# Top-k attention with two expert layers: the masks of six more heads move from VectorE to ScalarE

## Chip, cores and metric

One core of a Trainium2 chip runs the whole program. The metric is the device time of one execution in microseconds (us); lower is better.

## What is computed

The reference is attention that keeps only the 32 largest scores of each row, and then two dense layers with experts:

```
scores = q @ k^T / 8                              # 2 batches, 8 heads, 576 rows, head size 64
kth    = the 32nd largest score of each row
p      = exp(score - row max) where score >= kth, else 0
x      = (p / sum(p)) @ v                         # 1152 tokens x 512
x      = sum over 4 experts e: gate[:, e] * (relu(x @ w1[e]) @ w2[e])     # 512 -> 1024 -> 512
out    = max(x @ m1, x @ m2, x @ m3) @ mo                                 # 512 -> 768 -> 512
```

All of it is float32.

## The kernel before

**Attention.** The 1152 tokens are nine tiles of 128 rows; the heads go by twos, so there are 36 pairs, numbered here from 0 as in the code (the change's description counts from 1). A pair has a first head (j = 0) and a second head (j = 1). For each head TensorE makes scores (line 420 or 425), ScalarE copies them out of PSUM into `s` (line 432), and VectorE counts the 32 largest in seven instructions: four MAX8 into `m` (line 445), each giving eight values, and three MATCH_REPLACE8 into `work` (line 447). ScalarE keeps minus the maximum as `nb` (line 452).

**The mask** is lines 459 to 485. A head that ScalarE does not mask first has its whole row exponentiated by ScalarE (line 459, `p<-s,nb`). Then VectorE compares, multiplies and sums in one instruction (line 473, `p<-s,m,p`, with both tensors in SBUF). A head that is listed in `ON_ACT` has no line 459; ScalarE makes the mask in three activations instead (lines 466, 467, 468) and an accumulator read: a leaky slope that leaves scores at or above the 32nd nearly at zero and makes the others hugely negative after the exp's scale, a [128,1] bias, and the exp with its sum. Before the change `ON_ACT` has all first heads from pair 2 on, and the second heads of pairs 2, 5 and 6. The second heads of pairs 0, 1 and 4 are masked by GpSimd, the other thirty by VectorE.

**After the mask** TensorE transposes `p` (lines 491 and 496, tile `psp`), ScalarE copies the result out (lines 494, 499, tile `pt`), `rs` gets a small guard (line 504), VectorE takes the reciprocal `rr` (line 510), ScalarE spreads it (`rb`, line 514), TensorE transposes that (`psr`, line 519) and multiplies with v (`psv`, lines 533 and 536), VectorE multiplies the two into `xt` (line 543), ScalarE rounds `xt` to `xh` (line 556) and GpSimd makes the rest `xl` (line 557).

**The dense layers** run each product in three passes of split operands (lines 682, 683, 684). A weight block arrives as `raw`; ScalarE rounds it to `whi` (line 271) and GpSimd subtracts to get `wlo` in two halves (line 277). Hidden tiles `h` are split by ScalarE and VectorE (lines 824, 826), every fourth by ScalarE and GpSimd (lines 817 to 819).

**What sets the order.** Every engine runs its own instructions in the order in which the program issues them. The program is written in slots: pair n starts at slot 8n, its first head counts in slots 8n to 8n+6, its second `stag` slots later. A set of offsets (`FIRST`, `MIDDLE`, `TIGHT`, `SECOND`, `THIRD`, `LOOSE`, chosen by `options(n)`, line 566) says in which slot each step is issued. Pairs from 8 on use `LOOSE`, only pair 11 uses `THIRD`. In `LOOSE` VectorE's mask of the second head is in slot 8n+11 and ScalarE's mask of the first head in 8n+9 (`MASK_LATE` = 2). After each slot the dense layers, the filler of TensorE, are issued until their estimated TensorE time has caught up with the estimated VectorE time of the slots so far (`clock`); the mask on VectorE adds about 0.67 us to that estimate (`dve(S)`, line 472), and a mask on ScalarE adds none. TensorE's work in all is the same however it is divided between slots.

Of the kernel before, what the change touches and what calls it, by code (L numbers as in the profile page):

```python
# [31 lines left out]
ON_POOL = ((0, 1), (0, 1, 4))  # L32
W_AHEAD = 4
WIDE, W_FROM, W_STEP = 4, 306, 2
ON_ACT = (range(2, 36), (2, 5, 6))
STEEP = 2.0 ** 100
MASK_LATE = 2

FIRST = dict(stag=2, new=1, scores=-12, trans=11, pv=17, rec=16, lag=2, sum=4, late=1)
MIDDLE = dict(stag=2, new=1, scores=-12, at=(11, 12), pv=14, rec=12, lag=1, sum=0, late=1)  # L40
TIGHT = dict(stag=3, new=1, scores=-7, at=(10, 11), guard=11, rec=11, spread=12, pv=12, turn=12, norm=13, split=13, last=14, lag=0, lag_s=1, sum=0, late=1)
SECOND = dict(TIGHT, norm=14, split=14, last=15)
THIRD = dict(stag=4, new=1, scores=-4, at=(11, 12), guard=12, rec=13, spread=13, pv=14, turn=14, norm=15, split=15, last=16, lag=0, lag_s=2, sum=0)
LOOSE = dict(stag=4, new=1, scores=-4, trans=10, pv=17, rec=15, lag=2, sum=0)

EARLY = 7
# [13 lines left out]
def kernel(  # L60
# [15 lines left out]
    B, HP, D, _, S = k.shape  # L76
# [34 lines left out]
    at = ctx.enter_context(tc.tile_pool(name="at", bufs=2))  # L111
# [287 lines left out]
    class Pair:  # L399
        def __init__(self, n):  # L400
# [8 lines left out]
            self.on_pool = [n in ON_POOL[j] for j in range(2)]  # L409
            self.on_act = [n in ON_ACT[j] for j in range(2)]  # L410

# [147 lines left out]
    def attention():  # L559
# [3 lines left out]
        later, between = {}, {}  # L563

        def options(n):
            return TIGHT if n == HP - 1 else SECOND if n == 2 * HP - 1 else MIDDLE if n in (HP - 2, 2 * HP - 3, 2 * HP - 2) else FIRST if n < 2 * HP else THIRD if n == 3 * HP - 1 else LOOSE

        def at_slot(s, f, *a):
            later.setdefault(s, []).append((f, a))
# [3 lines left out]
        for n, (c, hp, t) in enumerate(pairs):  # L573
            for b in batches(t):
                if ("v", b, hp) not in first_use:
                    first_use["v", b, hp] = n
                    at_slot(8 * n + (options(n)["pv"] - 7 if b and hp else 0), load_v, b, hp)
                if t >= FULL:
                    first_use.setdefault(("k", b, hp), n)
            if t >= FULL:  # L580
                first_use.setdefault(("q", c, hp), n)
            elif n:
                o = options(max(0, n - 2))
                at_slot(max(8 * n + options(n)["scores"] - LOAD_FULL, 8 * (n - 2) + o["scores"] + o["stag"] + 1), load_full, n)
        free = {"k": -99, "q": -99}
        for key, n in first_use.items():
# [4 lines left out]
            at = max(s0 + options(n)["scores"] - (SPLIT_K if key[0] == "k" else SPLIT_Q), free[key[0]] + 2)  # L591
            if key[0] == "k" and key[1] and key[2]:

                at = max(at, 8 * pairs.index((MIXED, key[2] - 1, MIXED)) + options(n)["scores"] + options(n)["stag"] + (1 if key[2] == HP - 1 else 4))
# [3 lines left out]
        for n, (c, hp, t) in enumerate(pairs):  # L598
# [7 lines left out]
            for j in range(2):  # L606
# [9 lines left out]
                late = o.get("late", MASK_LATE) * pr.on_act[j]  # L616
# [40 lines left out]
    lag = []  # L657
# [439 lines left out]
```

## Time and profile before

| | us |
|---|---|
| median of three executions | 767.23 |
| lowest and highest of them | 760.99, 768.05 |
| the profiled execution, its own time | 766.07 |
| its span, first to last instruction | 764.2 |
| TensorE (PE) busy in the span | 731.3 |
| VectorE (DVE) busy | 621.3 |
| ScalarE (ACT) busy | 488.5 |
| GpSimd (POOL) busy | 462.3 |

How to read the rows: a row of the order of time gives the start in us from the span's start, how long it took, the engine, the line, the operation, output<-inputs with their sizes, and in brackets how long the engine had been idle in front of it and what ended that. PEld is TensorE's weight load, which runs beside matmuls. PEclk is the TensorE clock that was granted, 1.00 being 2.4 GHz and 0.50 being 1.2 GHz. A row of a stretch gives its ends, its length, and the busy time of PE, PEld, DVE, ACT and POOL, each with its number of instructions, then PEclk, the share of time that the DMA engines were busy, and GB/s. The attention lasts to about 462 us; behind it dense layers alone are left.

### The profile page before, as it was taken

The numbers are of one execution on the slowest core, as the hardware profiler recorded it, in microseconds if no ns is written. First come the engines' busy times: TensorE is split into PE (matmuls) and PEld (weight loads), VectorE is DVE, ScalarE is ACT, GpSimd is POOL, SyncE is SP. The second block draws the span as 40 slices with busy tenths as digits, with TensorE's granted clock in tenths as the row PEclk, the third lists the DMA queues.
The fourth block names the chain that finished last, engine by engine and source line by source line (L and its number), as shares of the span: only waits on it lengthen the run. The fifth ranks groups of instructions, "written<-read, shape, count | busy, mean of one in ns | idle before, by whom it ended". The sixth has DMA issues, their size and how long they took to land.

```text
span 764.2 us, 13550 instructions
## 1 busy us (share of the span) xinstructions
PE 731.3 (96%) x4678; PEld 644.8 (84%) x4678; DVE 621.3 (81%) x1172; ACT 488.5 (64%) x1109; POOL 462.3 (60%) x401
## 2 busy tenths in 40 slices
PE   6899999699999998999999999999999999999998
PEld 3576788588899897988998877899998899999996
DVE  6999989959999899999999996999999954233341
ACT  4668888647888885987885756576555633433431
POOL 2514789449989885796975405677686742442520
PEclk9999999889999999999999999999999999999999
DMA  7683565425755534354452666878877752453501
GB/s 217 186 268 139 159 194 151 132 63 172 199 149 166 166 118 144 102 165 152 145 152 90 204 251 234 277 241 280 259 260 227 241 172 85 135 183 97 192 2 42
DMA packets 56485, 130.14 MB, mean 170 GB/s; under 512 B 9761, under 2 KB 23329, under 8 KB 56417
## 3 DMA queue, kind: packets, MB, share of 16 engines
q1 hardware_dynamic: 48064, 120.69, 50.2%
q10 hardware_dynamic: 8352, 8.59, 3.2%
q8 instruction: 37, 0.61, 0.3%
q14 instruction: 32, 0.25, 0.1%
HBM read 120.60 MB, written 8.65 MB: 169 GB/s over the span
## 4 chain that ended last, share of the span: by engine, by line
PE 65%; DVE 17%; ACT 8%; issue 5%; POOL 4%; DMA 0%; ACTq 0%; POOLq 0%; DVEq 0%
PE ps L682 16%; PE ps L684 16%; PE ps L683 16%; DVE m L445 8%; DVE work L447 6%; PE psv L536 2%; POOL wlo L277 2%; PE pss L425 2%; ACT whi L271 2%; PE psp L491 2%; PE pso L683 2%; PE pso L682 2%; PE psa L767 2%; PE pso L684 2%; PE pss L420 1%
## 5 line engine op out<-in xcount | busy, mean ns | idle before, releaser
L277 POOL TENSOR_TENSOR wlo<-raw,whi 128x512 fp32r<-128x512 f32 x228 | 305.7, 1368 | 107.5 <-ACT whi L271 102.8
L271 ACT ACTIVATE whi<-raw 128x1024 fp32r<-128x1024 f32 x148 | 152.6, 1056 | 33.3 <-POOL narrow L248 16.3
L682 PE MATMUL ps<-xl,whi 128*128 128x256 f32 (+1 forms) x520 | 160.5, 309 | 0.2
L684 PE MATMUL ps<-xh,wlo 128*128 128x256 f32 (+1 forms) x520 | 156.6, 301 | 0.1
L683 PE MATMUL ps<-xh,whi 128*128 128x256 f32 (+1 forms) x520 | 156.4, 301 | 0.0
L445 DVE MAX8 m<-work 128x8 f32<-128x576 f32 x216 | 155.1, 744 | 0.1
L447 DVE MATCH_REPLACE8 work<-m,work 128x576 f32<-128x576 f32 x144 | 106.6, 741 | 0.0
L682 PEld LDWEIGHTS ps<-xl,whi 128*128 128x128 f32 x520 | 98.4, 189 | 1.9 <-POOL xl L557 0.6
L683 PEld LDWEIGHTS ps<-xh,whi 128*128 128x128 f32 x520 | 97.8, 188 | 1.3 <-issue 0.7
L684 PEld LDWEIGHTS ps<-xh,wlo 128*128 128x128 f32 x520 | 97.6, 188 | 0.3 <-POOL wlo L277 0.3
L277 DVE TENSOR_TENSOR wlo<-raw,whi 128x1024 fp32r<-128x1024 f32 x34 | 55.1, 1622 | 48.8 <-ACT whi L271 35.9
L682 PE MATMUL ps<-wlo,h 128*128 128x512 f32 x160 | 67.7, 423 | 7.5 <-POOL wlo L277 7.5
L248 POOL TENSOR_TENSOR narrow<-narrow,raw 128x256 int32<-128x256 int32 x48 | 47.1, 982 | 38.0 <-DVE narrow L245 13.0
L684 PE MATMUL ps<-whi,h 128*128 128x512 f32 x160 | 64.3, 402 | 2.0 <-POOL h L819 2.0
L683 PE MATMUL ps<-whi,h 128*128 128x512 f32 x160 | 64.0, 400 | 0.0
L432 ACT ACTIVATE s<-pss 128x288 f32<-128x288 f32 x144 | 51.2, 401 | 14.6 <-PE pss L420 11.3
L445 DVE MAX8 m<-s 128x8 f32<-128x576 f32 x72 | 53.8, 748 | 5.5 <-ACT s L432 5.5
L447 DVE MATCH_REPLACE8 work<-m,s 128x576 f32<-128x576 f32 x72 | 53.3, 741 | 0.0
L494 ACT ACTIVATE pt<-psp 128x512 f32<-128x512 f32 x72 | 42.7, 594 | 12.2 <-PE psp L491 11.9
L491 PE MATMUL psp<-ident,p 128*128 128x128 f32 x288 | 43.8, 281 | 5.4 <-POOL p L477 4.1
L684 PE MATMUL ps<-x2h,wlo 128*128 128x384 f32 x144 | 48.7, 338 | 0.0
L682 PE MATMUL ps<-x2l,whi 128*128 128x384 f32 x144 | 48.7, 338 | 0.0
(118 smaller groups left out, 1616.1 us busy)
## 6 DMA issues: line engine op xcount, KB each, us to landing
raw<-in_w_dram SPq DMA_DIRECT2D x112, 512.0 KB, 4.2
raw<-narrow SPq DMA_DIRECT2D x36, 512.0 KB, 3.4
whole<-in_w_dram SPq DMA_DIRECT2D x30, 512.0 KB, 5.9
raw<-in_m_dram SPq DMA_DIRECT2D x36, 256.0 KB, 4.3
narrow<-narrow ACTq DMA_DIRECT2D x48, 128.0 KB, 4.3
kraw<-in_k_dram SPq DMA_DIRECT2D x16, 288.0 KB, 4.5
qraw<-in_q_dram SPq DMA_DIRECT2D x48, 64.0 KB, 3.8
raw<-in_mo_dram SPq DMA_DIRECT2D x12, 256.0 KB, 4.1
```

What stands on the lines that cost most here:

```text
L248: nc.gpsimd.tensor_tensor(out=out.bitcast(I32), in0=out.bitcast(I32), in1=last, op=ALU.add)
L271: nc.scalar.activation(out=hi, in_=raw, func=AF.Copy)
L277: on.tensor_tensor(out=lo[:, x], in0=raw[:, x], in1=hi[:, x].bitcast(F32), op=ALU.subtract)
L425: nc.tensor.matmul(ps[:, 0:SH], lhsT=l, rhs=r, start=i == 0, stop=i == len(mm) - 1)
L432: nc.scalar.activation(out=s[:, h, :], in_=halves[h][:, 0:SH], func=AF.Copy)
L445: nc.vector.max(m[:, 8 * r:8 * r + 8], src)
L447: nc.vector.match_replace(out=self.w[j], in_to_replace=m[:, 8 * r:8 * r + 8], in_values=src, imm_value=NEG)
L491: nc.tensor.transpose(ps[:, r * P:(r + 1) * P], self.p[:, part, part * TAIL + r * P:part * TAIL + (r + 1) * P], ident)
L494: return lambda: [nc.scalar.activation(out=d, in_=ps.rearrange("p (r n) -> p r n", r=NR), func=AF.Copy), self.did.add(("pt", part))]
L682: nc.tensor.matmul(ps, lhsT=lh, rhs=rl, start=first, stop=False)
L683: nc.tensor.matmul(ps, lhsT=lh, rhs=rh, start=False, stop=False)
L684: nc.tensor.matmul(ps, lhsT=ll, rhs=rh, start=False, stop=last)
```

## The change

Six second heads are added to `ON_ACT`: those of pairs 8, 9, 10, 12, 13 and 14. These pairs get a set of offsets of their own, `BOTH`. It is `LOOSE` with `late=1`, so that both masks are issued one slot later than a VectorE mask would be (first head in slot 8n+8, formerly 8n+9; second head in 8n+12, formerly 8n+11 on VectorE), and the transposes stay where they were (`at=(13, 14)`). Pairs 11 and 15 keep their VectorE masks. The added line moves every later line number by one.

```diff
-ON_ACT = (range(2, 36), (2, 5, 6))
+ON_ACT = (range(2, 36), (2, 5, 6, 8, 9, 10, 12, 13, 14))
...
+BOTH = dict(stag=4, new=1, scores=-4, at=(13, 14), pv=17, rec=15, lag=2, sum=0, late=1)
 LOOSE = dict(stag=4, new=1, scores=-4, trans=10, pv=17, rec=15, lag=2, sum=0)
...
         def options(n):
-            return TIGHT if n == HP - 1 else SECOND if n == 2 * HP - 1 else MIDDLE if n in (HP - 2, 2 * HP - 3, 2 * HP - 2) else FIRST if n < 2 * HP else THIRD if n == 3 * HP - 1 else LOOSE
+            return TIGHT if n == HP - 1 else SECOND if n == 2 * HP - 1 else MIDDLE if n in (HP - 2, 2 * HP - 3, 2 * HP - 2) else FIRST if n < 2 * HP else THIRD if n == 3 * HP - 1 else BOTH if n in ON_ACT[1] else LOOSE
```

VectorE's order around the mask of pair 10's second head (`m_1500` before, `m_1493` after), before:

```order
L445 MAX m_1500<-work 128x8
L826 SCALAR_TENSOR_TENSOR h<-ps_1570,h 128x512
L447 MATCH_REPLACE work<-m_1602,work 128x576
L473 SCALAR_TENSOR_TENSOR p,rs<-s,m_1500,p 128x576
L445 MAX m_1702<-s 128x8
L445 MAX m_1602<-work 128x8
L543 TENSOR_TENSOR xt<-psv,r 128x128
```

After:

```order
L446 MAX m_1493<-work 128x8
L448 MATCH_REPLACE work<-m_1561,work 128x576
L446 MAX m_1673<-s 128x8
L446 MAX m_1561<-work 128x8
L544 TENSOR_TENSOR xt<-psv,r 128x128
L827 SCALAR_TENSOR_TENSOR h<-ps_1595,h 128x512
```

The mask between the last count of the head and `xt` is gone, and one split of a hidden tile has moved behind `xt`.

ScalarE's order at the same place, from the last `whi` ahead of `xh` to the mask of pair 11's first head (`m_1602` before, `m_1561` after), before:

```order
L271 ACTIVATE whi<-raw 128x1024
L556 ACTIVATE xh<-xt 128x128
L504 ACTIVATE rs<-rs 128x2
L452 ACTIVATE nb<-m_1702 128x1
L432 ACTIVATE s<-pss 128x288 x2
L494 ACTIVATE pt<-psp 128x512
L514 ACTIVATE rb<-rr 128x128
L494 ACTIVATE pt<-psp 128x512
L499 ACTIVATE pt_1742<-psp 128x128
L466 ACTIVATE s<-s,m_1602 128x576
```

After:

```order
L272 ACTIVATE whi<-raw 128x1024
L825 ACTIVATE h<-ps_1595 128x512
L467 ACTIVATE s<-s,m_1493 128x576
L468 ACTIVATE nb<-m_1493,nb 128x1
L469 ACTIVATE p,rs<-s,nb 128x576
L557 ACTIVATE xh<-xt 128x128
L272 ACTIVATE whi<-raw 128x1024
L505 ACTIVATE rs<-rs 128x2
L453 ACTIVATE nb<-m_1673 128x1
L433 ACTIVATE s<-pss 128x288 x2
L495 ACTIVATE pt<-psp 128x512
L515 ACTIVATE rb<-rr 128x128
```

The three activations of the new mask stand directly in front of `xh`, and one more `whi` follows it.

TensorE's order behind the transpose `psr` of pair 10, up to the first matmul that uses the `wlo` of the next weight block (`wlo_1814` before, `wlo_1830` after), before:

```order
L519 MATMUL psr_1793<-ident_87,rb_1770 128x128
L682 MATMUL ps2_1688<-wlo_1814,h_1601 128x512
L683 MATMUL ps2_1688<-whi_1813,h_1601 128x512
L684 MATMUL ps2_1688<-whi_1813,h_1601 128x512
L491 MATMUL psp_1837<-ident_87,p_1730 128x128 x4
```

After:

```order
L520 MATMUL psr_1790<-ident_87,rb_1760 128x128
L683 MATMUL ps2_1771<-wlo_1589,h_1473 128x512
L684 MATMUL ps2_1771<-whi_1588,h_1473 128x512
L685 MATMUL ps2_1771<-whi_1588,h_1473 128x512
L683 MATMUL ps2_1771<-wlo_1589,h_1473 128x512
L684 MATMUL ps2_1771<-whi_1588,h_1473 128x512
L685 MATMUL ps2_1771<-whi_1588,h_1473 128x512
L492 MATMUL psp_1817<-ident_87,p_1713 128x128 x4
L683 MATMUL ps2_1715<-wlo_1830,h_1646 128x512
```

Six matmuls with weights that are already there, and the transposes of pair 11's first head, now stand in front of it.

## Rows read from the trace of the kernel before

**Rows 1.** The profile's page: busy time of each engine in the span

```profile
PE 731.3 (96%) x4678; PEld 644.8 (84%) x4678; DVE 621.3 (81%) x1172; ACT 488.5 (64%) x1109; POOL 462.3 (60%) x401
```

**Rows 2.** Busy time by stretch: PE, PEld, DVE, ACT, POOL, then PEclk

```profile
95.00:134.50 39.50, 36.67 (x280) 33.12 (x281) 35.47 (x75) 33.64 (x75) 35.94 (x30) 1.00 0.55 172
134.50:165.00 30.50, 22.71 (x132) 18.38 (x132) 21.74 (x39) 13.56 (x39) 13.04 (x13) 0.83 0.41 116
165.00:205.00 40.00, 38.17 (x284) 34.68 (x283) 38.63 (x80) 33.62 (x75) 35.91 (x32) 1.00 0.52 144
...
290.00:300.00 10.00, 7.81 (x35) 5.87 (x34) 9.20 (x19) 7.45 (x15) 7.18 (x6) 0.83 0.56 177
...
460.00:764.20 304.20, 300.67 (x1585) 275.57 (x1583) 197.67 (x271) 144.32 (x259) 161.04 (x125) 1.00 0.55 182
```

**Rows 3.** TensorE in order of time, 122 to 154 us

```profile
122.91 0.50 PE L684 MATMUL ps<-whi,h 128*128 128x512 f32 x1 [1.74 <-POOL h L819]
...
140.46 0.63 PE L491 MATMUL psp<-ident,p 128*128 128x128 f32 x4 [0.69 <-DVE p L473]
141.89 0.33 PE L496 MATMUL psp<-ident,p 128*128 128x128 f32 x1 [0.80 <-DVE xt L543]
...
142.29 0.39 PE L683 MATMUL ps<-whi,h 128*128 128x512 f32 x1
142.53 0.39 PE L684 MATMUL ps<-whi,h 128*128 128x512 f32 x1
...
146.46 0.49 PE L533 MATMUL psv<-pt,v_last 128*128 128x128 f32 x2 [0.94 <-ACT pt L499]
...
153.59 0.79 PE L682 MATMUL ps<-wlo,h 128*128 128x512 f32 x1 [5.36 <-POOL wlo L277]
```

**Rows 4.** Busy time of two short stretches, columns as in rows 2

```profile
148.20:153.60 5.40, 0.04 (x2) 0.01 (x1) 4.57 (x11) 4.78 (x10) 3.29 (x4) 0.55 0.01 2
153.60:159.00 5.40, 5.40 (x15) 4.20 (x16) 2.14 (x6) 0.69 (x2) 3.63 (x3) 0.50 0.37 116
```

**Rows 5.** GpSimd in order of time, 133 to 153 us

```profile
133.96 2.54 POOL L277 TENSOR_TENSOR wlo<-raw,whi 128x512 fp32r<-128x512 f32 x2
...
137.16 2.54 POOL L277 TENSOR_TENSOR wlo<-raw,whi 128x512 fp32r<-128x512 f32 x2
...
152.26 1.27 POOL L277 TENSOR_TENSOR wlo<-raw,whi 128x512 fp32r<-128x512 f32 x1
```

**Rows 6.** ScalarE in order of time, 141 to 151 us

```profile
141.87 0.31 ACT L556 ACTIVATE xh<-xt 128x128 fp32r<-128x128 f32 x1 [5.51 <-DVE xt L543]
...
145.45 0.31 ACT L514 ACTIVATE rb<-rr 128x128 f32<-128x128 f32 x1 [1.99 <-DVE rr L510]
...
150.87 1.04 ACT L271 ACTIVATE whi<-raw 128x1024 fp32r<-128x1024 f32 x1
```

**Rows 7.** VectorE in order of time, 106 to 146 us

```profile
106.66 0.81 DVE L473 SCALAR_TENSOR_TENSOR p<-s,m,p 128x576 f32<-128x576 f32 x1
...
134.73 5.58 DVE L473 SCALAR_TENSOR_TENSOR p<-s,m,p 128x576 f32<-128x576 f32 x1
...
141.57 0.27 DVE L543 TENSOR_TENSOR xt<-psv,r 128x128 f32<-128x128 f32 x1
...
145.26 0.15 DVE L510 RECIPROCAL rr<-rs 128x2 f32<-128x2 f32 x1
```

**Rows 8.** VectorE's masks (line 473) alone, busy time by stretch, then PEclk

```profile
100.00:146.00 46.00, 8.05 (x6) 1.00 0.66 197
160.00:205.00 45.00, 4.23 (x6) 1.00 0.49 139
```

**Rows 9.** ScalarE in order of time: a mask, an exp, and what follows

```profile
103.24 0.78 ACT L466 ACTIVATE s<-s,m 128x576 f32<-128x576 f32 x1
...
105.01 0.76 ACT L459 ACTIVATE p<-s,nb 128x576 f32<-128x576 f32 x1
105.67 1.05 ACT L271 ACTIVATE whi<-raw 128x1024 fp32r<-128x1024 f32 x1
```

## The prediction made before the result was known

> **What bounds the kernel now.** I read the page first: TensorE is busy 96% of the span and no other engine over 81% [rows 1]. TensorE's work is the same before and after the change, so time can only be won where TensorE stands idle or runs at the lower clock. I then looked for those places by stretches. Behind the attention, from 460 us on, TensorE is busy 300.67 of 304.20 us [rows 2]: nothing to win. The stretch from 134.5 to 165 us stands out: TensorE is busy 22.71 of 30.50 us, idle 7.79, at a mean granted clock of 0.83 [rows 2]. Its neighbours lose 2.83 us (95 to 134.5) and 1.83 us (165 to 205), both at clock 1.00. A smaller dip of the clock lies in 290 to 300 us [rows 2].
>
> Third, TensorE in order of time through that stretch: four gaps of 0.69, 0.80, 0.94 and 5.36 us, together 7.79 [rows 3]. The first ends with VectorE's mask, the second with VectorE's `xt`, the third with a ScalarE copy, the fourth with a `wlo` from GpSimd. In the fourth TensorE does 0.04 us of work in 5.40, and the 5.40 us behind it run at clock 0.50, which is 1.2 GHz [rows 4]: 2.7 us of work at 2.4 GHz, so another 2.7 us lost. The stretch loses 7.79 + 2.7 = 10.5 us.
>
> Fourth, what lies behind these gaps, followed backwards. GpSimd makes the awaited `wlo` in 152.26 to 153.53, after its `whi` of 150.87 [rows 5, 6]. ScalarE is late with that `whi` because it stood 5.51 us in front of `xh` waiting for VectorE's `xt`, and 1.99 us in front of `rb` waiting for VectorE's `rr` [rows 6]. VectorE is late with both because one mask, that of pair 10's second head, took 5.58 us, from 134.73 to 140.31 [rows 7]. GpSimd subtracts without a pause nearly as long, from 133.96 to 139.70 [rows 5], and the mask ends 0.61 us after it. Pair 8's mask, undisturbed, takes 0.81 us [rows 7]: I take 5.58 - 0.81 = 4.77 us as waiting for GpSimd. This mask is one of the six that leave VectorE.
>
> The Trainium skill has a rule on such a meeting (page "SBUF — State Buffer", section "SBUF: two separate sides"): a VectorE instruction with two SBUF inputs and a GpSimd instruction that reads SBUF exclude each other, and whichever starts first keeps the shared ports for its whole instruction. The trace agrees that the mask is held up, but it was held through several GpSimd instructions, not one; the measurement decides here.
>
> **The change, part by part.**
>
> *Removed from VectorE.* Six masks with their accumulator reads: 8.05 us for the three of pairs 8 to 10 and 4.23 us for those of pairs 12 to 14 [rows 8], 12.3 us of busy time. VectorE's chain up to `xt` and `rr` of pair 10 gets shorter by the whole mask and its read, 140.24 - 134.73 = 5.51 us (the next instruction starts at 140.24, 0.07 us before the mask's recorded end).
>
> *Added to ScalarE.* Three activations and a read in place of one exp. Start to start, the mask in the trace is 105.01 - 103.24 = 1.77 us and the exp 105.67 - 105.01 = 0.66 us [rows 9]: 1.11 us more per head, 6.7 us over six. For pair 10 it stands in front of `xh`, where ScalarE waited 5.51 us: hidden there. If that cover is gone it costs its 1.11 us.
>
> *The large gap.* With `xt` and `rr` earlier by 5.51, ScalarE's run to `whi` moves likewise; one more copy (`pt`, about 0.5 us) now stands ahead of that `whi`. The first half of `wlo` ends at 153.53 - 5.51 + 0.5 = 148.5. TensorE, without the three small gaps (2.43 us), would come to it at 148.2 - 2.43 = 145.8, but has six more matmuls in front, 0.24 us apart [rows 3], so at 147.2. A gap of 1.3 us stays. The clock: the gap of 1.74 us at 122.9 [rows 3] lies in a stretch at clock 1.00 [rows 2], so I take it that 1.3 us leaves the clock up and the 2.7 us come back. Gain: 7.79 - 1.3 + 2.7 = 9.2 us. Bounds: if only the three small gaps go, 2.43; if everything goes, 10.5.
>
> *Pairs 8 and 9.* In 95 to 134.5 ScalarE is busy 33.64 of 39.5 us [rows 2] and feeds GpSimd, which ends the 1.74 us gap [rows 3]. Two masks of 1.11 us land here: between 0 and 2.2 us on the path. For the other sign, one of the two removed masks lies beside GpSimd work of which TensorE waits, worth at most that gap of 1.74. I take a loss of 1.1, half of what is added, because ScalarE's 5.9 us of idle time in 39.5 hides some of it.
>
> *Pairs 12 to 14.* Between everything idle there coming back (1.83 us [rows 2]) and three additions on the path (3.3 us). ScalarE has 6.4 idle us in that stretch, so I take 0.
>
> *New waits.* ScalarE's mask waits for the last MAX8 of its head. Queued behind it are `xh`, the next `whi` and `h`; GpSimd and TensorE wait for these. But `xt`, for which `xh` waits anyway, stands behind that MAX8 with three VectorE instructions between, so I count the wait at nothing. It costs if ScalarE gets there long before the count is done (last rival).
>
> *Pacing.* Six times 0.67 us less of estimated VectorE time: 4.0 us of TensorE work are issued later. In a span with TensorE busy at 96% this moves work and makes none: 0. It does shift every later meeting of engines, though. The dip near 290 us lost 10 - 7.81 = 2.19 us idle and 1.7 us by the clock (0.17 x 10) [rows 2]; it may go or come twice: 3.9 us either way, taken as 0.
>
> **Sum**, against the profiled execution's own 766.07 us: 766.07 - 9.2 + 1.1 = 758.0 us. That execution lies 1.16 us under the median of 767.23; a median after the change would be 758.0 to 759.1. I take 758.5. About 1%, 7.7 us here, is what a measurement of this kernel can tell from no change; the bound of "faster" is 759.6, that of "slower" 774.9.
>
> **Rivals.**
>
> *The gap stays where it is.* Only the gaps that end with VectorE go; `wlo` is late anyway, because ScalarE has the copies, a mask, an exp and a hidden tile between two `whi`, and the clock falls again. For it: GpSimd had nothing from `whi` for 12.6 us, 139.70 to 152.26 [rows 5]. Against: 7.5 of these are ScalarE's two waits [rows 6]. Time 766.07 - 2.43 = 763.6.
>
> *The hold-up moves to a mask that remains.* Pair 11 and pair 15 keep theirs on VectorE; with GpSimd fed more densely, the next one can be held like that of pair 10. For it: the six masks took from 0.81 to 5.58 us, so meetings are common. Against: five of the six, 12.28 - 5.58 = 6.7 us, took 1.3 us on average [rows 7, 8]. Time: 758.0 + 4.77 = 762.8. By the skill's rule, one GpSimd instruction (1.27 us [rows 5]) would be the most it could cost, and the time 759.3.
>
> *More goes.* The shift also removes the dip near 290 us: 758.0 - 3.9 = 754.1. For it: nothing but that the order there is different; against the same.
>
> *Slower: ScalarE becomes the engine that everything waits for.* Its masks stand in front of `whi`, in order; for pair 8 the first head's mask also moves ahead of two `whi`. If ScalarE arrives there before VectorE's count, it waits, `whi` is late, GpSimd and TensorE after it. Price: six additions of 1.11 us fully on the path, 6.7, with the present gap kept and one more spell at half clock (2.7): 766.07 + 9.4 = 775.5, on the median's level 776.6. It decides once additions and waits exceed ScalarE's idle time in 95 to 134.5, 5.9 us, that is from 3.7 us of new waits on over the 2.2 added. Against it: ScalarE is busy only 13.56 of 30.50 us in the stretch behind [rows 2].
>
> **How the numbers follow.** The forecast has 0.46, with an own range of 754 to 762 by the bounds of its terms; about two thirds of that is under 759.6. More goes: 0.12. The gap stays: 0.20. The hold-up moves: 0.12. Slower: 0.10. Faster by over 1%: 0.46 x 0.7 + 0.12 = 0.44. Slower by over 1%: 0.10. Within 1%: the rest, 0.46. The low end takes the larger gain with 2 us of room, 752; the high end takes the two cases near 763 on the median's level, 764.8, and 3.3 us for pairs 12 to 14, 768. Left out are the slower case and a tail below.
>
> **What would show it right or wrong.** Right: no VectorE mask over 2 us between 95 and 205 us; TensorE idle under 3 us between 134 and 165 with the clock at 1.00; ScalarE's waits for `xt` shorter than 2 us there. The step on pairs 8 and 9 is wrong if TensorE loses over 4 us in 95 to 134. The sum is wrong if a gap of several us in front of a `wlo` matmul appears elsewhere, or if ScalarE shows idle time in front of line 467 that VectorE ends: then the new wait is real.

## The result, and the profile after

Four runs of the changed kernel have a median of 756.98 us (755.58 to 760.3), beside 767.09 us (760.99 to 768.05) of four runs of the kernel before. The ratio is 0.9892, with a 95% interval of 0.986 to 0.9925: 1.1% faster. The forecast was 758.5 us. The number is nearly right; its composition, as the rest shows, is not. Every ratio, here and in the experiments, is taken against executions of the kernel before on the same chip (medians 767.09 us for the change, 766.73 for experiments 1 to 4, 766.96 for 5 to 8, 764.86 for 9 to 12), so experiments are compared by their ratios. A ratio leaves out executions over 1.5% slower than the fastest of the same kernel (two each in experiments 4 and 6), which the medians include.

The profiled execution of after took 756.88 us with a span of 755.1 us, 9.1 us less than the span of before. Page of after, busy time and chain by engine:

```profile
PE 729.3 (97%) x4678; PEld 645.8 (86%) x4678; DVE 610.3 (81%) x1160; ACT 495.3 (66%) x1127; POOL 458.1 (61%) x401
...
PE 90%; ACT 3%; DVE 2%; POOL 2%; issue 2%; DMA 0%; POOLq 0%; ACTq 0%
```

VectorE has 11.0 us less than in [rows 1] (12.3 were expected to go), ScalarE 6.8 us more (6.7 expected): the edit does what it says. TensorE's busy time fell by 2.0 us, its idle time (span less busy time) from 32.9 to 25.8 us, 7.1 less. Where the idle time went is read by stretch. Busy time of after, columns as in [rows 2]:

```profile
95.00:134.50 39.50, 36.49 (x261) 32.10 (x260) 32.87 (x69) 34.56 (x80) 31.04 (x27) 0.96 0.54 160
134.50:165.00 30.50, 26.10 (x165) 22.47 (x165) 20.96 (x48) 19.78 (x52) 18.02 (x19) 0.89 0.47 132
165.00:205.00 40.00, 39.40 (x303) 35.97 (x303) 38.25 (x81) 38.25 (x89) 35.47 (x32) 1.00 0.57 164
...
290.00:300.00 10.00, 10.00 (x73) 9.22 (x73) 10.00 (x25) 8.49 (x22) 6.86 (x7) 1.00 0.38 120
...
148.40:152.80 4.40, 0.02 (x1) 0.02 (x1) 1.91 (x5) 3.70 (x6) 2.56 (x3) 0.87 0.24 43
152.80:158.40 5.60, 5.60 (x18) 4.60 (x19) 1.58 (x4) 1.80 (x7) 4.09 (x4) 0.50 0.45 133
```

Against [rows 2]: the stretch that I had singled out, 134.5 to 165, gained 3.4 us of idle time (7.79 to 4.40); 165 to 205 gained 1.2; the dip of 290 to 300 us is gone, 2.2 us of idle time and a clock back at 1.00; 95 to 134.5 lost 0.2 and its clock fell to 0.96. Everything else together gained 0.5. The short stretches answer to [rows 4]: the large gap is still there, 4.4 us long, and 5.6 us behind it still run at clock 0.50. So the gap shrank and the clock behind it gave nothing back.

TensorE of after in order of time, at the two gaps over 1 us behind 95 us:

```profile
119.41 0.49 PE L534 MATMUL psv<-pt,v_last 128*128 128x128 f32 x2 [1.68 <-ACT pt L500]
...
147.78 0.60 PE L492 MATMUL psp<-ident,p 128*128 128x128 f32 x4
152.78 0.79 PE L683 MATMUL ps<-wlo,h 128*128 128x512 f32 x1 [4.40 <-POOL wlo L278]
153.37 0.63 PE L684 MATMUL ps<-whi,h 128*128 128x512 f32 x1
```

What TensorE does right ahead of the 4.40 us matters: four transposes `psp`. ScalarE of after over the same time:

```profile
136.54 0.77 ACT L467 ACTIVATE s<-s,m 128x576 f32<-128x576 f32 x1
...
138.30 0.29 ACT L557 ACTIVATE xh<-xt 128x128 fp32r<-128x128 f32 x1
...
146.59 0.28 ACT L522 ACTIVATE r<-psr 128x128 f32<-128x128 f32 x1 [0.75 <-PE psr L520]
148.42 0.60 ACT L495 ACTIVATE pt<-psp 128x512 f32<-128x512 f32 x1 [1.55 <-PE psp L492]
148.91 0.59 ACT L818 ACTIVATE raw<-ps 128x512 f32<-128x512 f32 x1
149.53 0.63 ACT L819 ACTIVATE h<-raw 128x512 fp32r<-128x512 f32 x1
150.07 1.99 ACT L272 ACTIVATE whi<-raw 128x1024 fp32r<-128x1024 f32 x2
```

and GpSimd:

```profile
150.24 1.26 POOL L820 TENSOR_TENSOR h<-raw,h 128x512 fp32r<-128x512 f32 x1 [4.27 <-ACT h L819]
151.47 2.50 POOL L278 TENSOR_TENSOR wlo<-raw,whi 128x512 fp32r<-128x512 f32 x2
```

Here `xh` no longer waits for `xt` at all (5.51 us in [rows 6]), and the mask in front of it starts without a wait. Yet `whi` starts at 150.07, only 0.80 us earlier than in [rows 6]. ScalarE has a new wait of 1.55 us: its copy `pt` needs the transposes that TensorE issues last before it stops. From there everything is in a row: `psp` ends at 148.38, `pt`, `raw`, `h` on ScalarE, `h` on GpSimd from 150.24, the first `wlo` from 151.47, and TensorE starts at 152.78. That row takes 4.40 us however early VectorE is.

### The profile page after: what moved, and what is told of

Read it like the earlier page. It is cut to its first block, busy times and chain, and to the rows that moved or that the text cites. A ratio compares the mean times of both kernels' runs of the same rounds, so it can differ in the third digit from the quotient of the medians.

```text
span 755.1 us, 13550 instructions
## 1 busy us (share of the span) xinstructions
PE 729.3 (97%) x4678; PEld 645.8 (86%) x4678; DVE 610.3 (81%) x1160; ACT 495.3 (66%) x1127; POOL 458.1 (61%) x401
## 4 chain that ended last, share of the span: by engine, by line
PE 90%; ACT 3%; DVE 2%; POOL 2%; issue 2%; DMA 0%; POOLq 0%; ACTq 0%
PE ps L683 20%; PE ps L684 20%; PE ps L685 20%; PE psv L537 5%; PE pss L426 4%; PE psp L492 4%; PE psa L768 2%; PE ps L804 2%; PE ps L845 2%; PE pso L684 2%; PE pso L683 2%; PE pso L685 2%; PE pss L421 2%; PE psv L534 1%; DVE m L446 1%
```

## The experiments

Two theories stood against each other. By the first, that of the prediction, the gain comes from pair 10's mask leaving VectorE, where GpSimd held it up (the hold-up). By the second it comes from the issue order: the planner counts a VectorE mask by `dve(S)` and lets TensorE run so much further ahead with its filler matmuls (layers of the experts); a ScalarE mask isn't counted, so six masks put off 4.0 us of TensorE's work, and all later meetings of engines shift (the order). Pair numbers in the edits count from 0: 8, 9, 10, 12, 13, 14. All twelve kernels compute the whole result.

**1. Only pair 10's mask moved.** Edit to the changed kernel:

```diff
-ON_ACT = (range(2, 36), (2, 5, 6, 8, 9, 10, 12, 13, 14))
+ON_ACT = (range(2, 36), (2, 5, 6, 10))
```

> Of the six masks only that of pair 10's second head is ScalarE's; the other five stay on VectorE. Hold-up theory (the gain comes from the one mask that GpSimd held for 4.8 us): TensorE's idle time from 134 to 165 us falls from 7.8 to about 4.4 us as in the full change, the time is 760 to 763, that is most of 3.4 us of the full change's 9 to 10. Load theory (six masks' worth of VectorE time, 12.3 us, is what counts): one sixth of the gain, 765. Order theory (the shift in the issue order, 4.0 us less of estimated VectorE time, moves later meetings of engines): one sixth of the shift, anything from 760 to 768, and the dip of the clock near 290 us stays.

Measured: 758.46 us, ratio 0.9903 (0.9876 to 0.9931). One of the six masks gives nearly the whole gain, which speaks for the first theory, but it also shifts the order. The dip near 290 us stayed (a gap of 2.41 us at 288.3), and two other masks were held up, at 202.0 and 319.0 us: here the hold-up did move to masks that remain. VectorE of this kernel, and GpSimd at the same time:

```profile
202.02 4.58 DVE L474 SCALAR_TENSOR_TENSOR p<-s,m,p 128x576 f32<-128x576 f32 x1
```

```profile
198.43 3.79 POOL L278 TENSOR_TENSOR wlo<-raw,whi 128x512 fp32r<-128x512 f32 x3
202.17 1.32 POOL L370 TENSOR_TENSOR ql<-qraw,qh 128x512 fp32r<-128x512 f32 x1
203.43 2.56 POOL L278 TENSOR_TENSOR wlo<-raw,whi 128x512 fp32r<-128x512 f32 x2
```

The mask ends 0.6 us after GpSimd's unbroken row of subtractions, as in [rows 5, 7].

**2. Only the order changed: all masks stay on VectorE, six aren't counted.** Edit to the kernel before:

```diff
             if not self.on_pool[j]:
-                dve(S)
+                if not (j and self.n in (8, 9, 10, 12, 13, 14)):
+                    dve(S)
```

> The kernel before, all masks where they were, but the six VectorE masks are not counted in the estimate that paces the dense layers, so that TensorE's order comes near that of the change. Hold-up theory: pair 10's mask is held again if it still meets a long run of GpSimd work, time 762 to 767; the dip near 290 us may go, worth 3.9 us. Load theory: no change, 766 to 767. Order theory: nearly the whole gain, 757 to 760, with masks of VectorE still in place.

Measured: 754.51 us, ratio 0.985 (0.9828 to 0.9872). In the traces TensorE's 4678 matmuls stand in the same order as in the change, by lines and operands. With not one mask moved, this is as fast as the change or faster. This felled the first theory as the main cause. VectorE, GpSimd and TensorE of this kernel:

```profile
132.84 1.04 DVE L474 SCALAR_TENSOR_TENSOR p<-s,m,p 128x576 f32<-128x576 f32 x1
```

```profile
129.46 5.58 POOL L277 TENSOR_TENSOR wlo<-raw,whi 128x512 fp32r<-128x512 f32 x4 [0.43 <-ACT whi L271]
```

```profile
149.51 0.80 PE L683 MATMUL ps<-wlo,h 128*128 128x512 f32 x1 [4.41 <-POOL wlo L277]
```

Pair 10's mask is still on VectorE and meets a row of GpSimd subtractions again, but takes 1.04 us, not 5.58 [rows 7]: it arrives at another moment and gets in between two of them. The large gap is 4.41 us, that of the change to 0.01. The dip near 290 us is gone.

**3. The change without its change of order: the six ScalarE masks are counted as before.** Edit to the changed kernel:

```diff
             if self.on_act[j]:
+                if j and self.n in (8, 9, 10, 12, 13, 14):
+                    dve(S)
                 eb = self.nb[j]
```

> The full change, but each of the six masks on ScalarE still counts 0.67 us in the estimate that paces the dense layers, so that no TensorE work is moved behind. Hold-up and load theory: the gain of the stretch 134 to 165 us stays, 757 to 761. Order theory: the gain goes, 764 to 767, and the dip near 290 us is back.

Measured: 764.02 us, ratio 0.9965 (0.9948 to 0.9983). TensorE's order is that of before but for 50 of its 4678 places: a mask of `BOTH` counts one slot later than before, so that a few scores and transposes pass filler matmuls (from 136 us on). The hold-up is gone here too, and the large gap is 3.47 us; still only a third of the gain appears. Part is given back at 189 us, and the dip near 290 stays. TensorE at 189 us, and the stretch:

```profile
189.11 0.79 PE L536 MATMUL psv<-pt,v_last 128*128 128x128 f32 x2 [2.13 <-ACT pt L502]
```

```profile
290.00:300.00 10.00, 9.13 (x62) 7.11 (x63) 8.29 (x19) 5.45 (x17) 6.39 (x7) 0.83 0.23 70
```

**4. Only the mask's slots changed: the offsets `BOTH` for the six pairs, masks on VectorE and counted.** Edit to the changed kernel, in which `options` now names the six pairs of `BOTH` by their numbers, since `ON_ACT` no longer lists them:

```diff
-ON_ACT = (range(2, 36), (2, 5, 6, 8, 9, 10, 12, 13, 14))
+ON_ACT = (range(2, 36), (2, 5, 6))
```

> The offsets BOTH for the six pairs, but the second heads' masks stay on VectorE in their old slot; what is left of the change is that the first heads' masks are issued one slot earlier. Hold-up and load theory: no gain beyond 1 us, 765 to 768, VectorE's mask of pair 10 held again or not by chance. Order theory: the pacing estimate is as before, so no gain either; a gain of over 4 us would say that the first heads' slot is what matters.

Measured: 770.59 us, ratio 1.0028 (1.0 to 1.0056). TensorE's order is that of before, and the slots alone gain nothing. VectorE of this kernel has the hold-up again:

```profile
135.11 5.36 DVE L474 SCALAR_TENSOR_TENSOR p<-s,m,p 128x576 f32<-128x576 f32 x1
```

**5. The hold-up by itself: as experiment 1, but pair 10's ScalarE mask is counted.** Edit to experiment 1:

```diff
             if self.on_act[j]:
+                if j and self.n == 10:
+                    dve(S)
                 eb = self.nb[j]
```

> Pair 10's second head alone goes to ScalarE and still counts in the pacing estimate, so TensorE's order is that of the kernel before. Hold-up theory: the 5 us hold-up and the long low-clock spell behind it are gone; idle time of TensorE from 134 to 165 us 3.5 to 4.5 instead of 7.8; time 758 to 761, as when this head was moved with its pacing. Order theory: the time stays within 2 us of before, 765 to 768, because the pacing, not the mask's engine, made the gain.

Measured: 763.17 us, ratio 0.9955 (0.9922 to 0.9989). TensorE issues in the order of before, but for one place at 136 us, where four score matmuls pass six of filler; otherwise only the mask that was held up has left: 3.5 us by the ratio (0.8 to 6.0 by its interval). In the profile the stretch and the gap are

```profile
134.50:165.00 30.50, 26.95 (x173) 23.17 (x172) 21.30 (x47) 19.43 (x50) 14.28 (x15) 0.89 0.42 117
```

```profile
148.70 0.79 PE L685 MATMUL ps<-wlo,h 128*128 128x512 f32 x1 [3.46 <-POOL wlo L278]
```

so 4.24 us of idle time came back there (7.79 to 3.55), and the clock still fell, to 0.89 in the mean. Experiment 1 (0.9903) differs from this one only in that the mask isn't counted: by the ratios, 0.67 us of filler put off made another 4 us (the two intervals just overlap).

**6. The order shifted behind the hold-up only: 4.0 us put off at slot 124.** Edit to the kernel before:

```diff
         before = clock["dve"]
+        if s == 124:
+            clock["goal"] -= 4.0
         while clock["pe"] < clock["goal"]:
```

> The kernel before, all masks on their engines and counted, but at slot 124 (pair 15) 4.0 us are taken off the goal that paces the dense layers: the same shift in all as the change makes, but behind the stretch with the hold-up. Order theory with two separate places: the stretch to 205 us is as before, with the hold-up, and only the dip near 290 us goes: 3.9 us less, 762 to 764. If the dip near 290 us has to do with the hold-up before it, no gain: 766 to 768.

Measured: 764.85 us, ratio 0.9976 (0.9934 to 1.0017): in time inconclusive. The trace is clear on one thing: the hold-up of 5.58 us is unchanged, and the dip near 290 us is gone:

```profile
290.00:300.00 10.00, 10.00 (x91) 9.05 (x90) 10.00 (x24) 8.09 (x21) 4.38 (x5) 1.00 0.24 78
```

A new gap of 1.41 us stands at 205.5 us, near the shift. So a shift of the order alone removes the dip.

**7. The order, three masks only (pairs 8, 9, 10 uncounted, all on VectorE).** Edit: as experiment 2, with `(8, 9, 10)`.

> The kernel before, but the masks of pairs 8, 9 and 10 alone are not counted in the pacing estimate (2.0 us), all on VectorE. Order theory: the stretch 95 to 165 us is that of the run with six uncounted (no long mask, idle 4.4 us in 134 to 165), worth 5 to 7 us; the dip near 290 us may stay, as half of the shift is missing: 758 to 762.

Measured: 760.34 us, ratio 0.9905 (0.9872 to 0.9938). Pair 10's mask takes 1.02 us and the large gap is 4.41 us, as with six; the dip near 290 is gone, but gaps of 2.02 us at 220.1 and 1.87 us at 456.0 are new. Half of the put-off work gives the early part of the gain and spoils some of it later.

**8. The change's TensorE order with all masks on VectorE: experiment 4 with the six masks uncounted.** Edit to experiment 4: that of experiment 2.

> TensorE's order is instruction for instruction that of the change, but the six masks are on VectorE; the only difference to the change is the engine of the masks. If the order makes the gain and three activations on ScalarE cost more than one VectorE instruction saves: 753 to 756, 1 to 3 us faster than the change, as with the six uncounted and the old offsets (754.5). If moving the masks off VectorE is itself worth something at this order: slower than the change, 759 to 762.

Measured: 755.57 us, ratio 0.9861 (0.9798 to 0.9924). TensorE issues what it issues in the changed kernel, instruction for instruction; only the engine of the six masks differs, and with it their slot. No mask is held up, the large gap is 4.41 us, the dip is gone. The change itself, at 0.9892 (0.986 to 0.9925), is not told apart from it. Two stretches of this kernel, for the comparison with after:

```profile
95.00:134.50 39.50, 37.09 (x278) 32.84 (x279) 36.88 (x77) 34.59 (x78) 34.71 (x29) 1.00 0.54 164
...
165.00:205.00 40.00, 38.52 (x297) 35.05 (x296) 38.99 (x83) 33.88 (x79) 35.84 (x30) 1.00 0.56 164
```

**9. How far the order carries: all VectorE masks from pair 8 on uncounted.** Edit: as experiment 2, with `range(8, 36)`.

> The kernel before with all 27 VectorE masks from pair 8 on left out of the pacing estimate (18 us of dense-layer work moved behind), none moved to another engine. If a smaller estimate is better as such, because it was too large: faster than with six left out (754.5), 749 to 753. If only the place of the meetings matters: anywhere between 752 and 766, with gaps of TensorE at other places than before. If too little is left for TensorE between the attention's steps: new idle time of TensorE in 205 to 440 us, over 5 us, and 760 or more.

Measured: 769.62 us, ratio 1.0078 (1.0045 to 1.0111): slower than before. The edit leaves 28 masks out, 18.8 us (the expectation is one short). The large gap grows to 5.75 us, and TensorE runs short of filler in the later attention. Stretch 310 to 440 us of this kernel, and then of after:

```profile
310.00:440.00 130.00, 126.10 (x927) 112.57 (x926) 129.03 (x276) 100.51 (x249) 91.34 (x82) 0.99 0.44 137
```

```profile
310.00:440.00 130.00, 130.00 (x970) 116.05 (x970) 128.10 (x277) 101.47 (x252) 88.25 (x80) 1.00 0.53 172
```

The attention ends earliest of all (the last pair's output is scaled at 446.7 us, 452.4 in after, 462.2 before), but what was put off is then done behind it: TensorE is busy 302.50 us from 460 us on, 291.50 in after.

**10 and 11. Twelve masks, on VectorE and on ScalarE.** Both issue TensorE's work in one order, that of twelve uncounted masks. Edit 10 is experiment 8 with the list `(8, 9, 10, 12, 13, 14, 15, 16, 17, 18, 19, 20)`; edit 11 puts the same list in `ON_ACT` of the changed kernel:

```diff
-ON_ACT = (range(2, 36), (2, 5, 6, 8, 9, 10, 12, 13, 14))
+ON_ACT = (range(2, 36), (2, 5, 6, 8, 9, 10, 12, 13, 14, 15, 16, 17, 18, 19, 20))
```

> Twelve masks (pairs 8 to 10 and 12 to 20) on VectorE but left out of the estimate, offsets BOTH for these pairs; TensorE's order is instruction for instruction that of the next run, where the same twelve masks are ScalarE's. Alone: 752 to 758. Against the next run: if three activations cost more than the VectorE instruction saves, this one is 2 to 5 us faster, twice what six made; if VectorE's time is worth anything at this order, it is slower.

> The change with six more second heads (pairs 15 to 20) on ScalarE. If the masks on ScalarE cost more than they save: 2 to 5 us slower than the run before with the same TensorE order, 756 to 762. If they save: faster than that run.

Measured: 760.51 us, ratio 0.9947 (0.9916 to 0.9978), on VectorE; 761.22 us, ratio 0.9959 (0.9929 to 0.9989), on ScalarE. The pair differs by 0.7 us in the median, while VectorE's busy time differs by 13.8 us (612.0 and 598.2). Where no mask is held up, it makes no measurable difference which of the two engines masks. That also answers the load theory of the expectations: taking this much off VectorE gains nothing measurable. Both are slower than six: TensorE's waits in front of `psv` for ScalarE's `pt`, 3.4 us from 95 to 460 us in after, come to 7.6 us (11 waits) in experiment 10 and 5.9 us (5 waits) in experiment 11.

**12. What is left of the large gap: experiment 2, with the hidden tile in front of that `wlo` split by VectorE instead of GpSimd.** Edit to experiment 2:

```diff
-            if ON_POOL_H and not count % ON_POOL_H:
+            if ON_POOL_H and not count % ON_POOL_H and count != 8:
...
-            dve(2 * N)
+            if count != 8:
+                dve(2 * N)
```

> Six masks left out of the estimate, on VectorE (754.5), and in addition the one hidden tile that GpSimd splits at 146 us is split by VectorE, with TensorE's order unchanged. Chain theory (the gap of 4.4 us that stays is a fixed chain: transposes, copy, two activations for the hidden tile, GpSimd's split of it, then the weight's split): the gap is shorter by GpSimd's 1.2 us at least, 2.7 to 3.3 us, and the time 752 to 754. If something else ends the gap, it stays at 4.4 us and the time at 754.5.

Measured: 753.39 us, ratio 0.9857 (0.9792 to 0.9922). TensorE of this kernel:

```profile
148.69 0.80 PE L683 MATMUL ps<-wlo,h 128*128 128x512 f32 x1 [3.47 <-POOL wlo L277]
```

The gap lost 0.94 us of 4.41, less than expected: it is that row of steps, but GpSimd's `h` (1.26 us in after) stood mostly beside `whi`. On this branch ScalarE also makes one activation for the tile instead of two, so `whi` starts 0.97 us behind `pt` instead of 1.66, and the first `wlo` 1.14 us behind `whi` instead of 1.41. In the time this isn't told apart from experiment 2. In the profiled executions the half-clock spell behind the gap was 6.8 us long here and 3.4 in experiment 2; but that is one execution of each, and the four of experiment 2 have mean granted clocks from 0.995 (755.11 and 756.65 us) to 0.998 (753.75 and 753.91 us). Experiments 2 and 12 have the lowest medians of all that ran, and beat the kernel before clearly. All their runs but one (753.1 to 755.11, and 756.65) lie below all runs of the change (755.58 to 760.3), but these ran on other chips and the intervals of the ratios overlap, so a lead over the change of 2 to 4 us is likely and not settled.

## Why the prediction came out as it did

The runs fill a table of two by two. Ratios to before:

| | six masks on VectorE | six masks on ScalarE |
|---|---|---|
| order of before | 1 (before); 1.0028 (exp. 4) | 0.9965 (exp. 3) |
| order of the change | 0.985 (exp. 2); 0.9861 (exp. 8) | 0.9892 (the change) |

Down a column is the order: 11.5 us on VectorE with the old offsets (before and exp. 2), 12.8 with `BOTH` (exp. 4 and 8), 5.6 us on ScalarE (0.9965 to 0.9892 of 767). Along a row is the engine: in the order of before 2.7 us against before, and 4.8 against experiment 4, which shares the offsets; nothing or a small loss in that of the change. The two overlap: in the new order VectorE's mask of pair 10 isn't held up, so moving it has nothing to win.

*The hold-up as the cause of the stretch's loss.* Right as far as it went: with pair 10's mask away and the order all but kept, 4.24 us of idle time came back there and 3.5 us in the time (exp. 5). That it needs ScalarE was wrong: uncounted, the mask takes 1.04 us on VectorE (exp. 2).

*The large gap: a gap of 1.3 us stays, the clock stays up, gain 9.2.* This step failed. 4.40 us stayed, the clock fell, and 3.4 us came back: TensorE stopped at 148.38 (I had 147.2) and started at 152.78 (I had 148.5). I let ScalarE's whole run up to `whi` move by VectorE's 5.5 us and noted only that one more `pt` stood ahead. But that `pt` reads the transposes `psp`, and TensorE's order, shown with the change, has `psp` directly in front of the awaited `wlo` matmul on TensorE. ScalarE can't pass `pt` before TensorE has run dry, and all steps from there to `wlo` lie in the gap: 4.40 us in the change, 4.41 in experiment 2. The rival "the gap stays where it is" named the copies and the hidden tile between two `whi`, which was the mechanism, though it kept 5.36 us.

*The clock.* From a gap of 1.74 us at clock 1.00 [rows 2, 3] I took it that short gaps cost no clock; in after a gap of 1.68 us at 119.4 was followed by 3.4 us at half clock. The gap of 1.3 us that I applied it to never came about.

*Pairs 8 and 9, a loss of 1.1.* Near in size, but made up otherwise: 0.2 us more idle time (39.50 - 36.49 = 3.01 against 2.83), and the clock at 0.96 for 39.5 us, 1.6 us, which I hadn't counted. Experiment 8, with the same TensorE order, is idle for 39.50 - 37.09 = 2.41 us: the order took 0.4 us off, and ScalarE's masks put 0.6 on. The gap that GpSimd's `h` ended in [rows 3] is gone, and one that ScalarE's `pt` ends (1.68 us) stands in its place.

*Pairs 12 to 14, 0.* The stretch gained 1.2 us of idle time (1.83 to 0.60). Without any mask moved, experiment 2 has 40.00 - 38.93 = 1.07 us idle there, and experiment 8, which shares the change's offsets too, 40.00 - 38.52 = 1.48: the order is worth 0.4 to 0.8 us of it, the masks' engine the rest, 0.5 to 0.9. What the engine gains here it about loses at pairs 8 and 9.

*New waits, 0.* Right: no mask on ScalarE in 95 to 205 us waits for VectorE, and its waits for `xt` there fell from 11.0 to 0.9 us. So the slower rival, which lives on these waits, had no start. The hold-up that moves to another mask didn't occur in the change (longest mask in 95 to 205: 1.66 us), but did in experiment 1.

*Pacing: "this moves work and makes none: 0".* This is the step that failed most. Putting off 4.0 us of TensorE's work alone gives 11.5 us by the ratio (exp. 2). It does three things: pair 10's mask meets GpSimd at a harmless moment, the dip near 290 us goes (2.2 us idle and 1.6 us by the clock), and 205 to 290 us runs almost without a gap (0.79 us idle before, 0.17 in exp. 2). I had seen the second and set it to nothing as a rival of 0.12 ("more goes"). That rival came true, with a smaller gain of the large gap beside it; the two errors, 9.2 taken for 3.4 and nothing taken for the dip and the rest, nearly cancel in 758.5. That the number came out near is luck.

*The sum.* Idle time accounts for 7.1 of the 9.1 us: 3.4 at 134.5 to 165, 2.2 at 290, 1.2 at 165 to 205, 0.3 elsewhere with its losses. The other 2.0 us are TensorE's busy time, in which the clock's spells and overlapping matmuls mix; they stay unassigned. On balance the clock gave nothing: from 95 to 460 us the half-clock spells hold 8.5 us of TensorE's busy time before and 9.1 in after, since the new one at 120.9 us stands for that of the dip.

What stays open: why six uncounted masks fit best. Three (0.9905), twelve (0.9947 and 0.9959) and all 28 (1.0078) are worse, each with gaps at other places. With all 28, TensorE runs short of filler; between three and six it seems a matter of which instructions meet, and no run shows a rule for it.

## What to carry to other kernels

Where an edit also changes an issue order (here by a planner that counts one engine's work), run the two apart, the move alone and the order alone; a small shift of filler work can be worth more than the move it came with. Before a wait is shortened on paper, go round the loop: if what the late engine does first needs the last thing that the waiting engine issues before it stops, the gap has a floor, the sum of the steps between them. An engine that is held up at one moment of a dense program may be freed by arriving at another moment, and the next edit may bring it back.

## What the runs showed of the hardware

*A VectorE mask and GpSimd's rows of subtractions.* The fourteen profiles hold 394 VectorE masks. All but five take at most 2.02 us; the five take 5.58 (before and exp. 6), 5.36 (exp. 4), 4.58 and 3.93 us (exp. 1). The rule of the Trainium skill (page "SBUF — State Buffer", section "SBUF: two separate sides"), that the one that starts first holds the shared ports for its whole instruction and the other blocks, fits the 389: undisturbed 0.81 us plus one GpSimd instruction of 1.27 is 2.08. It doesn't cover the five, which sat through four or five GpSimd instructions that followed each other without a pause. It isn't chance: before, experiment 4 and experiment 6 hold the same mask. What decides whether a waiting mask gets in at the next boundary no run here shows. In experiment 2 pair 10's mask started 1.9 us earlier (132.84, before 134.73), beside another GpSimd instruction, and got in at the end of that one.

*The clock after a gap.* Gaps of 1.74 us (before, at 122.9) and 2.12 us (exp. 11, at 119.2) were not followed by half clock; the gap of 1.68 us in after was, and so was one of 2.12 us in experiment 4 (at 196.7). Behind the large gap the half-clock spell was 10.2 us (before, gap 5.36), 6.8 us (after, 4.40; exp. 12, 3.47; exp. 5, 3.46) or 3.4 us (exp. 2, 4.41; exp. 3, 3.47). TensorE was busy for 3.1 to 5.8 us of these spells, so each cost between 1.6 and 2.9 us, and a gap's length alone doesn't tell which.
